# Output gates loaded with values and keys, POOL as a second DMA queue, and gate arithmetic in chunks of two

## The chip, the cores and the metric

The kernel runs on one core of a Trainium2 chip. Its time is the device time of one execution in microseconds (us). The engines of the core are named as the profile names them: PE is TensorE (PEld its weight loads), DVE is VectorE, ACT is ScalarE, POOL is GpSimd, SP is SyncE, which only issues DMAs here. Each engine works through its own instructions in the program's order and waits on semaphores for the others.

## The reference

An mLSTM-like attention over 4 batches, 8 heads and 768 steps with head size 40 is followed by a mixture of 8 experts, of which each of the 3,072 tokens takes two.

```python
for t in range(S):                                   # S = 768
    m_new = np.maximum(f_gate[:, :, t] + m, i_gate[:, :, t])
    f_stab = np.exp(f_gate[:, :, t] + m - m_new)
    i_stab = np.exp(i_gate[:, :, t] - m_new)
    C = f_stab * C + i_stab * outer(v_t, k_t)        # per batch and head, 40 x 40
    n = f_stab * n + i_stab * k_t
    denom = np.maximum(np.abs(n . q_t), 1.0)
    y[:, :, t] = sigmoid(o_gate[:, :, t]) * (C q_t) / denom
x = y as (3072, 320)
noisy = x @ w_gate + log1p(exp(x @ w_noise)) * noise
top2 of the 8 experts, weights softmax over the two
out[token] += weight * (relu(x @ w1[e]) @ w2[e])     # w1: 320 x 1024, w2: 1024 x 320
```

## The kernel before

The attention is done in chunks of 64 steps. A *unit* is one chunk of one pair of batches, so there are 2 x 12 = 24 units, and unit u gives 128 rows of x. The main loop runs over i = 0 to 23; iteration i finishes unit i and prepares units i+1 and i+2. The program's order is written out by hand, and a tile framework adds the semaphores.

In iteration i TensorE computes the state update (`c_part`, line 344), the output (`o_part`, line 353), the logits of the gates for unit i+2 (`e_part`, line 290, which reads the tiles LE and RE), the router's logits (line 398), the transpose of x of unit i-1 (`t_part`, line 378) and the scores of unit i+2 (`s_part`, lines 311 and 315, which read QK). ACT takes exponentials (line 293), the sigmoid of the output gate in place (`sig_part`, lines 298 to 300) and copies. DVE scales the keys (`k_part`, line 323, output kd), forms the weighted scores (`p_part`, lines 330 to 334) and divides by the denominator (`f_part`, lines 358 to 366, output tm). The product of tm with the sigmoid gives x (xr, line 367), on POOL up to unit 12 and on DVE after that.

Loads. `load_unit(u)` brings unit u into one of four buffers: queries and keys transposed (QK, line 141, two DMAs of 160 KB), values and keys in rows (VK, lines 143 and 144, two of 162 KB) and output gates (SG, line 146, one of 160 KB into one of five buffers). It is called for unit i+3 at the start of iteration i. `keep_rows(i-1)` then stores x of the unit before to a table in DRAM (line 370). All of these stand in SP's queue. So do the gates' rows: the recurrence of the forget and input gates is computed by DVE with scans along time (`gate_math`, lines 181 to 200) into the tile HL, first 128 steps, then 128, then 256 and 256 (the last 256 in portions of three instructions in iterations 1 to 3), and `gate_move` (lines 208 and 210, three DMAs for two units) brings HL's rows into LE and RE, every other iteration. From iteration 4 to 9 a piece of the first expert's w1 is loaded (lines 114 and 117) and from 6 to 11 split into a high and a low part by ACT and DVE (lines 133 and 134); pieces of w2 follow in iterations 13 to 16.

Before the loop TensorE runs 20 matmuls on zeros (`warm`, line 608), the scores of unit 0, four more on zeros, and the gates' logits of units 0 and 1. POOL blanks the rows of the four buffers that no load fills (`blank`, lines 160 to 163). ACT and DVE put columns of the identity into the buffers of units 0 to 3 (`keys`, lines 249 and 250). DVE makes a table of token numbers from constants (line 256).

From iteration 9 on groups of units are routed: DVE runs small steps between the others, and POOL scatters each token's number and weight into its expert's slots with indirect DMAs (line 562, two per unit). When 32 of them are issued (units 0 to 15), SP loads the first expert's slots (line 649), POOL gathers its tokens (line 663), TensorE transposes them (line 690), and the expert phase begins.

## Time and profile before

| | us |
|---|---|
| median of 3 runs | 587.41 |
| lowest, highest | 583.69, 587.6 |
| the profiled execution | 586.21 |
| its span, first to last instruction | 584.4 |

Busy time of the engines in the span: PE 547.4 (94%), PEld 497.5 (85%), DVE 341.3 (58%), ACT 252.0 (43%), POOL 226.5 (39%). TensorE's mean granted clock is 0.953 of the full speed. A matmul's end is modelled in the profile, so PE's share is not a measure of how much room is left; the stretches in which it waits are. Times of rows are counted from the span's start. The attention phase takes about the first quarter of the span, the eight experts the rest.

### The profile page before, as it was taken

To read this page: it belongs to the slowest core of one execution; us is meant where nothing else is said; L and a number is where in the kernel's file an instruction comes from. 1 tells how busy PE (TensorE), PEld (TensorE's weight loads), DVE (VectorE), ACT (ScalarE), POOL (GpSimd) and SP (SyncE) were. 2 spreads that over 40 slices of the span, in tenths; PEclk is the share of its full clock that TensorE was granted. 3 is DMA by queue.
4 is the path that set the end of the run, shared out by engine and by line. 5 is a ranking of instruction groups with operands and counts; after the bars stand their busy time and mean duration, and the time that the engine had idled before them with its cause. 6 is when DMAs were issued, how large, how long until landed. Compare 5 with 4: busy or idle time off the path is not lost. (4 is left out here: it accounts for less than half of the span.)

```text
span 584.4 us, 13268 instructions
## 1 busy us (share of the span) xinstructions
PE 547.4 (94%) x5098; PEld 497.5 (85%) x5099; DVE 341.3 (58%) x947; ACT 252.0 (43%) x612; POOL 226.5 (39%) x256
## 2 busy tenths in 40 slices
PE   8789888999799899999999999999999999999992
PEld 3678777888679798999899899989989988998992
DVE  8885648999774266663564465366356536635410
ACT  4667765877332154531551353254145225414300
POOL 7012111676545572434514424352442435241052
PEclk9789977999679799999999999999999999999997
DMA  6668887886273855544336345432634634241033
GB/s 163 154 167 229 220 223 203 239 208 165 84 252 112 268 73 138 153 109 67 76 102 148 50 139 135 48 91 82 148 61 125 144 42 128 48 45 14 1 41 37
DMA packets 47429, 72.07 MB, mean 123 GB/s; under 512 B 10290, under 2 KB 37115, under 8 KB 47344
## 3 DMA queue, kind: packets, MB, share of 16 engines
q1 hardware_dynamic: 35680, 54.36, 32.1%
q0 software_dynamic: 11680, 16.80, 18.2%
q8 instruction: 42, 0.69, 0.5%
q14 instruction: 27, 0.22, 0.1%
HBM read 53.47 MB, written 18.38 MB: 123 GB/s over the span
## 5 line engine op out<-in xcount | busy, mean ns | idle before, releaser
L858 POOL DMA_INDIRECT y_out<-y,mm x56 | 87.0, 1554 | 186.1 <-DVE y L848 185.4
L663 POOL DMA_INDIRECT xg<-rows,mm x56 | 58.5, 1044 | 61.0 <-DMA mm<-slots 30.2
L692 ACT ACTIVATE xh<-s 128x384 fp32r<-128x384 f32 (+1 forms) x56 | 25.9, 469 | 122.3 <-PE s L690 122.0
L817 PE MATMUL s<-xh,w1h 128*128 128x512 f32 (+1 forms) x255 | 77.8, 361 | 0.4 <-ACT xh L692 0.4
L823 DVE SCALAR_TENSOR_TENSOR hlo<-s,hh 128x512 fp32r<-128x512 f32 (+1 forms) x85 | 47.5, 559 | 43.6 <-ACT hh L822 43.2
L817 PE MATMUL s<-xh,w1l 128*128 128x512 f32 (+1 forms) x255 | 63.3, 357 | 0.0
L822 ACT ACTIVATE hh<-s 128x512 fp32r<-128x512 f32 (+1 forms) x85 | 41.8, 491 | 48.0 <-PE s L817 46.8
L562 POOL DMA_INDIRECT slots<-meta,ix x48 | 49.9, 1040 | 30.4 <-DVE ovm L557 16.6
L835 PE MATMUL o<-w2h,hh 128*128 128x320 f32 x176 | 55.7, 317 | 0.0
L835 PE MATMUL st<-w2h,hh 128*128 128x320 f32 x176 | 55.6, 316 | 0.0
L837 PE MATMUL st<-w2h,hlo 128*128 128x320 f32 x176 | 54.4, 309 | 0.0
L837 PE MATMUL o<-w2h,hlo 128*128 128x320 f32 x176 | 54.4, 309 | 0.0
L836 PE MATMUL st<-w2l,hh 128*128 128x320 f32 x176 | 54.4, 309 | 0.0
L836 PE MATMUL o<-w2l,hh 128*128 128x320 f32 x176 | 54.4, 309 | 0.0
L817 PEld LDWEIGHTS s<-xh,w1h 128*128 128x128 f32 x255 | 46.7, 192 | 6.7 <-ACT xh L692 0.6
L817 PEld LDWEIGHTS s<-xh,w1l 128*128 128x128 f32 x255 | 45.2, 191 | 5.8
L817 PE MATMUL s<-xl,w1h 128*128 128x512 f32 (+1 forms) x170 | 46.9, 357 | 0.0
L134 DVE TENSOR_TENSOR w1l<-raw,w1h 128x512 fp32r<-128x512 f32 (+1 forms) x48 | 33.3, 694 | 15.2 <-ACT w1h L133 14.5
L817 PE MATMUL e<-xh,w1h 128*128 128x320 f32 (+1 forms) x129 | 39.6, 361 | 0.0
L367 POOL TENSOR_TENSOR xr<-tm,sg 128x320 f32<-128x320 f32 x13 | 11.7, 904 | 68.6 <-DVE tm L366 20.1
L315 PE MATMUL s<-qk 64*64 64x64 f32 x768 | 36.6, 237 | 1.4 <-DMA qk<-qk_in 1.4
L353 PE MATMUL o<-vk,p 128*64 128x41 f32 (+2 forms) x768 | 32.3, 241 | 5.6 <-DVE p L334 3.6
(190 smaller groups left out, 1290.6 us busy)
## 6 DMA issues: line engine op xcount, KB each, us to landing
raw<-w_in SPq DMA_DIRECT2D x7, 1280.0 KB
vk<-vk_in SPq DMA_DIRECT2D x48, 162.0 KB
qk<-qk_in SPq DMA_DIRECT2D x48, 160.0 KB
raw<-w_in SPq DMA_DIRECT2D x7, 1024.0 KB
y_out<-zrow SPq DMA_DIRECT2D x15, 320.0 KB
raw<-w_in SPq DMA_DIRECT2D x18, 256.0 KB
sg<-og_in SPq DMA_DIRECT2D x24, 160.0 KB
rows<-xr SPq DMA_DIRECT2D x24, 160.0 KB
```

The source lines that it names most:

```text
L134: lo.tensor_sub(W1L[n, k, s], RAW1[n, k, s], W1H[n, k, s].bitcast(F32))
L315: T.matmul(SQ[u][p][half[p], h, :], q[r, 1, h, :], q[r, 0, h, :], start=True, stop=True)
L353: T.matmul(OQ[u][half[p], h, :], PP[u][p][n, h, :], VK[u % 4][p][n, h * 41:h * 41 + 41], start=True, stop=True)
L562: st = P.indirect_dma_start(out=MT, out_offset=bass.IndirectOffsetOnAxis(ap=ix[:, 2 * u + k:2 * u + k + 1], axis=0), in_=meta[:, u, k], in ...
L663: P.indirect_dma_start(out=XG[0:rows_of(t), t], out_offset=None, in_=XD[0:n], in_offset=bass.IndirectOffsetOnAxis(ap=token(e, t), axis=0), ...
L817: T.matmul(ps[:, 0:n], l, r, start=i == 0, stop=i == len(ops) - 1)
L822: A.activation(HH[:, f, c], ps[:, 0:m], AF.Relu)
L823: V.scalar_tensor_tensor(HLO[:, f, c], ps[:, 0:m], 0.0, HH[:, f, c].bitcast(F32), op0=OP.max, op1=OP.subtract)
L835: T.matmul(ps, HH[:, j, c], W2H[:, j], start=j == 0, stop=False)
L836: T.matmul(ps, HH[:, j, c], W2L[:, j], start=False, stop=False)
L837: T.matmul(ps, HLO[:, j, c], W2H[:, j], start=False, stop=j == 7)
L858: st = P.indirect_dma_start(out=out, out_offset=bass.IndirectOffsetOnAxis(ap=token(e, t), axis=0), in_=y[0:n], in_offset=None, compute_op= ...
```

## The change

Output gates no longer have a load of their own. A row of values and keys grows from 648 to 968 numbers and carries the gates of its half; the buffer of unit u is [128, 2, 968], and the gates are its columns 648 to 967 of the first part. So the gates have four buffers and not five, and the load of values and keys of unit i+3 overwrites the gates of unit i-1.

POOL's queue issues the moves of gates from the second on, up to iteration 12, and the stores of x of units 0 to 11; later ones stay on SP. Queries and keys of unit 0 are issued by ACT. The arithmetic of the gates is done by 128 steps throughout: 256 to 383 in iteration 0, 384 to 511 in iteration 1 and 512 to 767 in portions of four instructions in iterations 2 to 5. The identity columns of units 1 to 3 are put by POOL, those of unit 1 earlier than before, and POOL blanks the fourth buffer after the second move of gates. The four matmuls on zeros between the first scores and the first logits go. The pieces of w1 are loaded from iteration 6 and split from iteration 8, the pieces of w2 loaded from 14, and the zeros for the gathered rows written in iterations 6 to 12 (before: 4 to 10).

```diff
-W1LD, W1AT, W2AT = 4, 6, 13
+W1LD, W1AT, W2AT = 6, 8, 14
...
-    VKS = [att.tile([128, 2, 648], F32, name=f"vk{i}") for i in range(4)]
-    VK = [[t[:, p] for p in range(2)] for t in VKS]
-    SG = [att.tile([128, DM], F32, name=f"sg{i}") for i in range(5)]
+    VKS = [att.tile([128, 2, VW], F32, name=f"vk{i}") for i in range(4)]
+    VK = [[t[:, p, 0:648] for p in range(2)] for t in VKS]
+    SG = [t[:, 0, 648:VW] for t in VKS]
...
         if "v" in what:
-            SP.dma_start(VK[u % 4][0][0:64], vk[pr, c, 0])
-            SP.dma_start(VK[u % 4][1][64:128], vk[pr, c, 1])
-        if "o" in what:
-            SP.dma_start(SG[u % 5], og[:, u])
+            flat = VKS[u % 4].rearrange("p x c -> p (x c)")
+            SP.dma_start(flat[0:64, 0:VW], vk[pr, c, 0])
+            SP.dma_start(flat[64:128, 648:648 + VW], vk[pr, c, 1])
...
     blank(0, V)
+    load_unit(0, "k", A)
     blank(1, P)
...
     gate_move(0, (SP, P))
     blank(2, P)
-    blank(3, P)
...
     run(gate_math(GC * L, 256))
+    gate_move(1, (P, P))
+    blank(3, P)
     SP.dma_start(fit[:, :, 256:], fi[:, :, 256:])
     load_unit(1, "v")
-    load_unit(0, "o")
-    gate_move(1)
...
     keys(0, V, V)
+    keys(1, P, P)
...
     def keep_rows(u):
-        SP.dma_start(XD[128 * u:128 * u + 128], XR[u])
+        (P if u < XV - 1 else SP).dma_start(XD[128 * u:128 * u + 128], XR[u])
...
     s_part(0)
-    warm(WARM2)
     e_part(0, first=True)
     s_part(1)
     e_part(1, first=True)
-    keys(1, A, V)
     k_part(0)
     p_part(0)
-    keys(2, A, V)
-    keys(3, A, V)
+    keys(2, P, P)
+    keys(3, P, P)
...
         if i % 2 == 0 and i and i // 2 + 2 < 2 * GB:
-            gate_move(i // 2 + 2)
+            gate_move(i // 2 + 2, (P, P) if i < XV else (SP, SP))
...
         if i == 0:
-            run(gate_math(256, 512))
-            gate_move(2)
-            gates2 = gate_math(512, 768)
-        elif i < 4:
-            for _ in range(3):
+            run(gate_math(256, 384))
+            gate_move(2, (P, P))
+            gates2 = (s for t0 in (384, 512, 640) for s in gate_math(t0, t0 + 128))
+        elif i < 6:
+            for _ in range((8, 4, 4, 4, 4)[i - 1]):
                 next(gates2, None)
```

SP's queue in iteration 8 (the loads of unit 11) up to the first loads of iteration 9, before. The numbers behind the names are the buffers' own; qk_96 and vk_100 are the fourth buffers, raw holds the raw weights.

```order
L141 DMA qk_96<-qk_in 40x1024 x2
L143 DMA vk_100<-vk_in 64x648
L144 DMA vk_100<-vk_in 64x648
L146 DMA sg_102<-og_in 128x320
L370 DMA rows<-xr 128x320
L208 DMA le_87<-hl 32x2x64
L210 DMA re_85<-hl 1x16x128 x2
L114 DMA raw_113<-w_in 128x512
L141 DMA qk_93<-qk_in 40x1024 x2
```

And after, the same stretch:

```order
L143 DMA qk_96<-qk_in 40x1024 x2
L146 DMA vk_100<-vk_in 64x968
L147 DMA vk_100<-vk_in 64x968
L119 DMA raw_108<-w_in 64x512 x2
L143 DMA qk_93<-qk_in 40x1024 x2
```

The load of gates, the store of x and the three moves have left the queue, and the next unit's queries and keys follow the loads of this one and a piece of w1.

POOL's queue from the product of unit 7 to that of unit 9, before:

```order
L367 TENSOR_TENSOR xr<-tm,sg_103 128x320
L764 MEMSET xg 128x320
L367 TENSOR_TENSOR xr<-tm,sg_104 128x320
L764 MEMSET xg 128x320
L367 TENSOR_TENSOR xr<-tm,sg_105 128x320
```

And after:

```order
L370 TENSOR_TENSOR xr<-tm,vk_100 128x320
L766 MEMSET xg 128x320
L373 DMA rows<-xr 128x320
L212 DMA le_87<-hl 32x2x64
L214 DMA re_85<-hl 1x16x128 x2
L370 TENSOR_TENSOR xr<-tm,vk_97 128x320
L766 MEMSET xg 128x320
L373 DMA rows<-xr 128x320
L370 TENSOR_TENSOR xr<-tm,vk_98 128x320
```

The store of each unit and, in every other unit, three moves now stand between one product and the next.

POOL's queue at the start, after the blanking of the third buffer (vk_99), up to the first product, before:

```order
L160 MEMSET vk_100 32x328
L161 MEMSET vk_100 32x320
L162 MEMSET qk_96 32x1024
L163 MEMSET qk_96 32x1024
L255 MEMSET w1l 64x1024
L367 ISA
L367 TENSOR_TENSOR xr<-tm,sg_101 128x320
```

And after:

```order
L212 DMA le_88<-hl 32x2x64
L214 DMA re_86<-hl 1x16x128 x2
L162 MEMSET qk_96 32x1024
L163 MEMSET qk_96 32x1024
L164 MEMSET vk_100 32x328
L165 MEMSET vk_100 32x320
L251 COPY vk_98<-cs 40x320
L252 COPY vk_98<-cs 64x320
L251 COPY vk_99<-cs 40x320
L252 COPY vk_99<-cs 64x320
L251 COPY vk_100<-cs 40x320
L252 COPY vk_100<-cs 64x320
```

The second move of gates stands ahead of the fourth buffer's blanking, and the copies of identity columns (vk_98 is the buffer of unit 1, vk_100 that of unit 3) behind it; the memset of w1l and the first product follow.

## Rows read from the trace of the kernel before

**Rows 1.** Windows: us; busy PE, PEld, DVE, ACT, POOL; clock; DMA share; GB/s.
```profile
36.50:43.90 7.40, 6.01 (x121) 5.33 (x117) 5.70 (x13) 3.85 (x10) 0.87 (x1) 0.79 0.74 186
54.35:59.57 5.22, 4.73 (x121) 4.17 (x117) 2.22 (x6) 4.11 (x10) 1.18 (x2) 1.00 0.91 260
70.76:79.30 8.54, 6.20 (x121) 5.50 (x117) 4.40 (x11) 4.34 (x10) 1.17 (x2) 0.75 0.78 215
90.23:98.30 8.07, 7.69 (x111) 6.69 (x113) 7.91 (x43) 3.46 (x9) 1.24 (x2) 0.61 0.85 219
...
162.80:584.40 421.60, 407.15 (x2464) 379.40 (x2464) 213.35 (x514) 147.34 (x363) 160.88 (x178) 0.98 0.43 100
...
36.50:79.30 42.80, 35.92 (x787) 31.85 (x783) 26.09 (x62) 28.89 (x68) 7.93 (x13) 0.91 0.81 217
```

**Rows 2.** Waits of PE from 36.5 to 79.3: total us, times, longest.
```profile
PE s L311 <- DMA qk<-qk_in: 6.8, 6, 2.3
```

**Rows 3.** Timeline, units 8 and 9: start, us, engine; SP's issues, waiting scores.
```profile
68.78 0.79 SPq L141 DMA_DIRECT2D qk<-qk_in  x2
...
70.91 0.55 SPq L146 DMA_DIRECT2D sg<-og_in  x1
...
73.78 1.46 SPq L210 DMA_DIRECT2D re<-hl  x2
...
75.80 1.12 PE L311 MATMUL s<-qk,cs 64*64 64x512 f32 x2 [2.32 <-DMA qk<-qk_in]
...
76.22 0.98 SPq L141 DMA_DIRECT2D qk<-qk_in  x2
```

**Rows 4.** Timeline of PE at the start: first scores, first gate logits.
```profile
9.77 1.24 PE L315 MATMUL s<-qk 64*64 64x64 f32 x32 [1.36 <-DMA qk<-qk_in]
...
12.09 0.47 PE L290 MATMUL e<-re,le 98*128 98x512 f32 x1
```

**Rows 5.** Timeline of DVE at the start: gate arithmetic, constants, kd.
```profile
3.66 0.48 DVE L181 TENSOR_TENSOR_SCAN xg<-raw,xg 64x128 f32<-64x128 f32 x1
...
5.88 0.29 DVE L198 CAST hl<-xg 64x256 fp32r<-64x256 f32 x1
6.20 0.48 DVE L200 SCALAR_TENSOR_TENSOR hl<-hl,raw,xg 64x256 fp32r<-64x256 f32 x1
...
9.49 1.07 DVE L198 CAST hl<-xg 64x256 fp32r<-64x256 f32 x1
...
18.61 0.18 DVE L256 CAST toki<-cs 128x24 int32<-128x24 f32 x1 [2.16 <-DMA cs<-cst_in]
18.71 0.83 DVE L323 TENSOR_TENSOR kd<-vk,w 128x640 f32<-128x640 f32 x1
...
24.06 0.75 DVE L181 TENSOR_TENSOR_SCAN xg<-raw,xg 64x256 f32<-64x256 f32 x1
...
28.35 0.81 DVE L323 TENSOR_TENSOR kd<-vk,w 128x640 f32<-128x640 f32 x1
```

**Rows 6.** Timeline of POOL: a move of gates, memsets, a product, a long scatter.
```profile
7.00 0.73 POOL L210 DMA_DIRECT2D re<-hl  x1 [2.78 <-DVE hl L200]
...
9.47 0.94 POOL L163 MEMSET qk<- 32x1024 f32 x1
...
62.61 0.87 POOL L367 TENSOR_TENSOR xr<-tm,sg 128x320 f32<-128x320 f32 x1 [4.46 <-DVE tm L366]
63.41 0.38 POOL L764 MEMSET xg<- 128x320 f32 x1
...
108.37 1.61 POOL L562 DMA_INDIRECT slots<-meta,ix  x1 [0.31 <-issue]
```

**Rows 7.** Timeline of POOL at the end of the attention phase.
```profile
142.40 1.39 POOL L562 DMA_INDIRECT slots<-meta,ix  x1 [2.04 <-DVE ovm L557]
...
149.22 0.98 POOL L562 DMA_INDIRECT slots<-meta,ix  x1 [0.30 <-issue]
...
154.04 1.05 POOL L663 DMA_INDIRECT xg<-rows,mm  x1 [3.84 <-DMA mm<-slots]
```

More of the change, by code (lines that the diff above doesn't have):

```diff
@@ L46 @@
 GC = 2
+VW = 968
 KE = 98
-W1LD, W1AT, W2AT = 4, 6, 13
+W1LD, W1AT, W2AT = 6, 8, 14
 SC = ((20, 2), (NU, 3))
@@ L60, in build @@
 @with_exitstack
-def build(ctx, tc, qk, vk, og, fi, noise, wgn, w1, w2, cst, ce, rmask, vacant, out):
+def build(ctx, tc, qk, vk, fi, noise, wgn, w1, w2, cst, ce, rmask, vacant, out):
     nc = tc.nc
@@ L135, in split_w1, with load_unit @@
                 yield
-    def load_unit(u, what="kvo"):
+    def load_unit(u, what="kv", q=None):
         pr, c = divmod(u, NCH)
@@ L159, in blank @@
     def blank(i, q):
+        q.memset(QK[i][96:128], 0.0)
+        P.memset(QK[i][32:64], 0.0)
         P.memset(VK[i][1][32:64, 0:328], 0.0)
         P.memset(VK[i][0][96:128, 328:648], 0.0)
-        q.memset(QK[i][96:128], 0.0)
-        q.memset(QK[i][32:64], 0.0)
     blank(0, V)
+    load_unit(0, "k", A)
     blank(1, P)
@@ L169, in build @@
     SP.dma_start(cet, ce)
-    load_unit(0, "kv")
+    load_unit(0, "v")
     SP.dma_start(cs[:, C_CI:C_CI + 320], cst[:, C_CI:C_CI + 320])
@@ L182, in gate_math @@
         yield
-        gt = gts[t0 // 256 % 2][:, 0:n]
+        gt = gts[t0 // 128 % 2][:, 0:n]
         V.tensor_add(gt, f, mt[:, t0:t1])
@@ L189, in gate_math @@
         yield
-        ag = ags[t0 // 256 % 2][:, :, 0:n]
+        ag = ags[t0 // 128 % 2][:, :, 0:n]
         V.tensor_tensor_scan(ag[:, 1, :], rmt[:, 0:n], gt, 0.0, OP.mult, OP.add)
@@ L200, in gate_math @@
         V.scalar_tensor_tensor(HL[:, :, t0:t1], HL[:, :, t0:t1].bitcast(F32), rmt[:, 256:257], ag, op0=OP.mult, op1=OP.add)
+        yield
     GB = NCH // GC
@@ L295, in sig_part @@
     def sig_part(u):
-        g = SG[u % 5]
+        g = SG[u % 4]
         A.activation(g, g, AF.Exp, scale=-1.0)
@@ L366, in f_part @@
         V.tensor_mul(tm, ps[:, :, 0:D], dn[:, :, None].to_broadcast([128, H, D]))
-        (P if u < XV else V).tensor_mul(XR[u], tm.rearrange("p h d -> p (h d)"), SG[u % 5])
+        (P if u < XV else V).tensor_mul(XR[u], tm.rearrange("p h d -> p (h d)"), SG[u % 4])
     def keep_rows(u):
-        SP.dma_start(XD[128 * u:128 * u + 128], XR[u])
+        (P if u < XV - 1 else SP).dma_start(XD[128 * u:128 * u + 128], XR[u])
     XS = {}
@@ L762, in build @@
             next(pre1)
-        if 4 <= i < 11:
-            P.memset(XG[:, i - 4], 0.0)
+        if 6 <= i < 13:
+            P.memset(XG[:, i - 6], 0.0)
         for _ in range(at(SC, i)):
@@ L1050, in layout @@
         qk[:, :, 0, :, x] = a[:, :, 1]
-    vk = z(2, NCH, 2, L, 648)
+    vk = z(2, NCH, 2, L, VW)
     a = i["v"].reshape(2, 2, H, NCH, L, D).transpose(0, 3, 1, 4, 2, 5)
@@ L1054, in layout @@
     v[..., :D] = a
-    vk[..., :328] = v.reshape(2, NCH, 2, L, 328)
-    vk[..., 328:] = i["k"].reshape(2, 2, H, NCH, L, D).transpose(0, 3, 1, 4, 2, 5).reshape(2, NCH, 2, L, DM)
-    og = np.ascontiguousarray(i["o_gate"].reshape(2, 2, H, NCH, L, D).transpose(0, 1, 4, 3, 2, 5)).reshape(2, 128, NCH, DM)
-    og = np.ascontiguousarray(og.transpose(1, 0, 2, 3)).reshape(128, NU, DM)
+    k, og = [i[n].reshape(2, 2, H, NCH, L, D).transpose(0, 3, 1, 4, 2, 5).reshape(2, NCH, 2, L, DM) for n in ("k", "o_gate")]
+    for p in range(2):
+        vk[:, :, p, :, 320 * p:320 * p + 328] = v.reshape(2, NCH, 2, L, 328)[:, :, p]
+        vk[:, :, p, :, 320 * p + 328:320 * p + 648] = k[:, :, p]
+        vk[:, :, p, :, 648 * (1 - p):648 * (1 - p) + 320] = og[:, :, p]
     fi = np.stack([i["f_gate"].reshape(2, 1, 16, S), i["i_gate"].reshape(2, 1, 16, S)], 3)
```

5 lines of the change are left out of this document (2 added, 3 removed).

## The prediction

> **What bounds the kernel now.** I read the span by windows first, cut where a unit's output matmuls (line 353) begin, then the waits of TensorE, then the queue that the waits point to. From 162.8 us on, the expert phase runs 421.6 us with TensorE busy 407 and the clock at 0.98 [rows 1]. The change touches nothing there, so it can only move the point where that phase begins. Before it stand 24 attention units. A unit in which TensorE hardly waits costs 4.73 us of its work at the full clock (the window from 54.35: busy 4.73 of 5.22). But the seven units from 36.50 to 79.30 took 42.80, which is 6.11 each. In them TensorE waited six times, 6.8 us together, and each time for queries and keys still in flight [rows 2]. The two worst (windows from 36.50 and 70.76, 7.40 and 8.54 us) also ran at a mean granted clock of 0.79 and 0.75, so matmuls cost more as well. Seven units at 4.73 would be 33.1: 9.7 us lie here, 6.8 in waits and 2.9 in clock and small waits.
>
> Why are the loads late? The SP queue issues everything, in order. One turn begins with the two qk loads of unit 11 at 68.78, and those of unit 12 begin at 76.22: 7.44 us a turn, against 4.73 that TensorE needs [rows 3]. The first four issues took 2.13 us (68.78 to 70.91). The sg load, the x store, the three moves of gates and a piece of w1 fill the other 5.3, waits among them. In such a turn SP falls behind TensorE, and at 75.80 TensorE has stood 2.32 us for the qk issued at 68.78.
>
> **The change part by part.**
>
> *SP's queue, units 3 to 9.* The sg load goes into the vk rows, and the store of x and three moves of gates every other unit go to POOL. Per unit SP keeps four issues (2.13 us) and in six units a piece of w1 (two issues at most, as long as two qk: 0.79), 2.9 us against 4.73. It then waits for buffers to come free. The new wait is that vk of unit i+3 overwrites the gates of unit i-1, so it needs POOL's product xr of unit i-1; the next unit's qk is queued behind it. That product began at 62.61 and took 0.87 [rows 6] in unit 7, so vk of unit 11 could be issued at 63.5 and qk of unit 12 about 1.2 us later, where they went out after 69.57 and at 76.22 [rows 3]. The wait added thus ends 6 us before the issue of that vk and 11 before that of the qk in the old order, and the user of that qk comes two units later. I therefore let all six waits go: up to -9.7. What is next late? DVE has 26.1 us of work in these 42.8 [rows 1]; the gates' steps of units 3 to 5 (four steps each, about 1.5 us) bring a DVE turn near 4.85, 0.1 a unit over TensorE. The transfers: a unit moves 320 + 484 + 160 KB, 0.99 MB, and 1.25 with a piece of w1, which at the 260 GB/s of the best window [rows 1] is 4.80 us. Both take back 0.7 together. Term: **-9.0**, between -3.0 (transfers stay slow, below) and -9.7.
>
> The Trainium skill's "Perfetto Trace Analysis", section "What 'DMA-bound' means", lists the DMA engines and the issuing sequencer as two different bounds. SP's 7.44 us a turn speak for the sequencer, and the DMA share of 0.81 in the same stretch says that the engines are not far from it [rows 1, 3]; by the first the term is -9.0, by the second its small end.
>
> *Start, units 0 to 2.* Queries and keys of unit 0 leave on ACT's queue, the four extra warm matmuls go, the identity columns of units 1 to 3 and the second move of gates go to POOL. TensorE's first scores started at 9.77 after 1.36 of waiting for qk, and the first e matmul at 12.09 [rows 4]. Without the wait and the 1.04 us of warm matmuls both come about 2 us earlier. That is not yet the end's gain, because DVE is next. It waited 2.16 us for constants that stood behind the gates and sg on SP (line 256, 18.61), then did kd of unit 1 at 18.71 [rows 5]. Those stood behind an sg load (0.55) and three moves (1.46 for two) [rows 3] that now leave SP, so they come 2 to 2.5 us earlier. But kd of unit 1 waits for POOL: three moves of gates from about 11, at 0.73 (the one that POOL issues already) to 0.98, with 0.30 of issue [rows 6, 7], so 3.1 to 3.8; the blanking of the fourth buffer, two memsets of 0.94 and two near 0.38 [rows 6], 2.6; two copies of 320 columns, which no row of POOL shows, between the 0.38 of a memset as wide and the 0.87 of a product with two inputs [rows 6], so 0.8 to 1.8. End: 17.5 to 19.2; I take 18.0, as a copy reads one input only: 0.7 earlier. Then the gates' arithmetic: a chunk of 256 held DVE from 24.06 to 28.35, 4.29 us; one of 128 went from 3.66 to 6.68, 3.0 [rows 5]. So kd of unit 2 gains another 1.3. A whole chunk of 128 after unit 1 takes 3.0 where three of the eight steps of 256 took 1.6 in proportion, which gives 1.4 back, hidden in part by TensorE. Over all 24 units DVE does four chunks of 3.0 where there were two of about 4.2, 3.6 us more, spread over six units; of it I count only what the unit times above hold. Term by the start of unit 3: **-1.2**, range 0 to -2.5.
>
> *POOL.* It takes over 12 stores and 8 moves of three: 36 DMAs. Nothing in the trace shows such a store on POOL. The nearest rows are its scatter of 128 rows, 0.98 with 0.30 idle before it, 1.61 at worst, and its direct move, 0.73 [rows 6, 7]. At 1.28 a pair of units costs POOL two products of 0.87, two memsets of 0.38 in units 6 to 12 and five DMAs: 8.9 us of the 9.46 that TensorE takes for two. So they fit, with little room, and xr of the even units comes about 1.4 us later than its inputs. TensorE reads that xr a unit later, after some 3 us more. Price: 0; it becomes a rival if a DMA costs more. The scatters themselves begin later, at unit 13, and the stores are back on SP then.
>
> The Trainium skill's "SBUF — State Buffer", section "Who interferes with whom", says that a DVE copy or cast in its fast mode and a GpSimd operation shut each other out for the whole instruction, descriptor writing included, which speaks against moving work to POOL. The trace agrees that they collide: the cast of one chunk took 0.29 alone and 1.07 when it started with POOL's memset of 0.94 [rows 5, 6]. By that rule each of the 36 DMAs could wait for a cast of at most 0.3 to 0.4 us, in the few units that have one; the sum stays, since POOL's 0.5 us of room per pair covers it.
>
> *Pieces of w1 two units later.* Their splitting on DVE (0.7 each for 512 columns, in proportion to kd's 0.83 for 640 [rows 5]) now falls on units 12 and 13, in the stretch from 90.23 where DVE was busy 7.91 of 8.07 us [rows 1]. One piece lands in a unit with idle DVE, one not: **+0.5**, between 0 and +1.4. The half-speed clock there (0.61) stays.
>
> *The end of the attention phase.* The experts' first gather began at 154.04. It waits for the last of six scatters, issued at 149.22; the first of these, at 142.40, had POOL idle for 2.04 us until DVE's routing of units 13 to 15 was done [rows 7]. So the gather follows the units, with 2.04 us to spare over POOL's earlier scatters, and moves with them.
>
> **Sum:** -9.0 - 1.2 + 0.5 = -9.7. The profiled execution took 586.2 us, its span 584.4; 586.2 - 9.7 = 576.5. The runs shown have a median of 587.4 (583.7 to 587.6), and the profiled one stands 1.2 below it; I split the difference: **577 us**. About 1%, 5.9 us, is what a measurement of this kernel can tell from no change.
>
> **The rivals.**
>
> 1. *The transfers are the bound, not SP's issue.* The same bytes must pass, and the stretch moved them at 217 GB/s with the engines 0.81 busy [rows 1]. If units 6 to 11 with w1 stay at that rate, a unit takes 1.25 MB / 217 = 5.75 us, 6 x 1.0 more than forecast: 583. For it: the qk issued at 68.78 had not landed 6 us later, with other loads beside it [rows 3]. Against it: 260 GB/s in one window, and larger rows in place of the sg rows of 1,280 bytes.
>
> 2. *POOL becomes the bound, and the time ends above the old one.* If a DMA on POOL costs d, a pair costs 2.5 + 5d; it exceeds 9.46 from d = 1.39, and eats the whole 9.7 us over five and a half pairs from d = 1.74. With d = 2.0, the worst scatter and its issue (1.61 + 0.30 [rows 6, 7]) rounded up, it is 12.5 a pair, +3.0 x 5.5 = +16.7: 593. xr then holds up vk, and qk behind it. For it: nine tenths of POOL are filled by the plan already, and a move that waits for TensorE to be done with the gates' buffer keeps the next xr behind it. Against it: 0.73 for the one direct move in the trace.
>
> 3. *The waits only move, to DVE.* The chunk after unit 1 and the four steps after each of units 2 to 5, stretched by POOL as the cast of 1.07 was [rows 5], hold five units at 5.4 in place of 4.85: 2.8 less gained, and the start gives nothing, another 1.2: 581. For it: DVE works 26.1 of 42.8 us already [rows 1]; against it, that leaves 2.4 us a unit.
>
> **How the numbers follow.** Forecast 0.58 (its own range is 572 to 580.5; the low end is 577 with the start at -2.5, nothing given back by w1, and the unit from 90.23 at the full clock, some 3 us), rival 1 0.20, rival 3 0.09, rival 2 0.12, and 0.01 for anything else. The range of 571 to 587 takes in rivals 1 and 3 and leaves out rival 2 and the edges. Faster by over 1% means below 581.5: the forecast and most of rival 3, 0.65. Within 1%: rival 1, the rest of rival 3 and what is left over, 0.23. Slower: rival 2, 0.12.
>
> **What would show it.** Right: the windows of units 4 to 10 near 4.8 us at clock 1.00, no wait of the scores' first matmuls (line 311) for qk above 0.3 us, SP waiting for POOL's xr; kd of unit 1 near 18, of unit 2 near 26; POOL's store near 1 us; the gather at about 144.5. Wrong: POOL stores of 1.5 us or more, with t of a unit waiting for xr; qk waits that persist with the DMA share above 0.9; or kd of unit 1 held by POOL's copies beyond 19.

## The result, and the profile after

The changed kernel takes 579.94 us (median of 6 runs, 577.32 to 583.08), the kernel before, in as many runs beside it, 586.69 (583.69 to 590.77). The ratio is 0.9883 with a 95% interval of 0.9835 to 0.9932: 6.8 us faster, where 577 had been forecast. The profiled execution took 578.57 us with a span of 576.7, against 586.21 and 584.4. Lines of the changed kernel stand one to three higher than before: output 356 (353), scores 314 and 318 (311 and 315), logits 293 (290), kd 326 (323), xr 370 (367), store 373 (370).

Where the 7.7 us of the two spans come from, read at the starts of the output matmuls of units 3, 10, 14 and 23 and of the experts' first matmul:

| stretch | before | after | difference | forecast |
|---|---|---|---|---|
| start to unit 3 | 36.50 | 40.28 | +3.8 | -1.2 |
| units 3 to 9 | 42.81 | 33.97 | -8.8 | -9.0 |
| units 10 to 13 | 24.00 | 22.36 | -1.6 | } +0.5 |
| units 14 to 22 | 46.28 | 47.74 | +1.5 | } |
| unit 23 to the experts | 13.22 | 12.87 | -0.4 | 0 |
| experts | 421.6 | 419.5 | -2.1 | 0 |

The windows of the changed kernel, cut as in [rows 1], with two more: 12 to 26, and the first 4.2 us of the experts (columns: us; busy PE, PEld, DVE, ACT, POOL; clock; DMA share; GB/s).

```profile
0.00:40.28 40.28, 30.95 (x438) 22.22 (x440) 29.15 (x80) 20.30 (x40) 23.41 (x42) 0.79 0.78 176
12.00:26.00 14.00, 10.89 (x167) 8.69 (x168) 8.08 (x23) 7.42 (x15) 8.99 (x15) 0.55 0.94 194
40.28:74.24 33.96, 33.41 (x784) 29.59 (x781) 25.13 (x64) 27.00 (x64) 16.06 (x28) 1.00 0.88 247
85.12:91.85 6.73, 6.35 (x111) 5.60 (x113) 6.67 (x39) 3.65 (x10) 3.84 (x8) 0.75 0.64 180
157.20:161.40 4.20, 4.20 (x19) 3.41 (x19) 3.59 (x13) 1.53 (x5) 3.29 (x4) 1.00 0.51 178
157.20:576.70 419.50, 404.81 (x2464) 377.67 (x2463) 213.53 (x514) 146.88 (x363) 160.98 (x178) 0.98 0.43 100
```

The kernel before, in three stretches that were not shown:

```profile
0.00:36.50 36.50, 28.82 (x441) 20.04 (x444) 31.00 (x75) 21.58 (x43) 13.80 (x23) 0.91 0.64 157
12.00:26.00 14.00, 10.12 (x194) 8.36 (x194) 11.01 (x29) 8.89 (x19) 3.69 (x4) 0.80 0.80 184
162.80:167.00 4.20, 4.20 (x11) 3.33 (x12) 1.89 (x9) 0.98 (x4) 3.08 (x4) 0.50 0.61 206
```

In units 3 to 9 TensorE is now busy 33.41 of 33.96 us at the full clock, and the waits for queries and keys [rows 2] are gone. This is the whole list of PE's waits there that count:

```profile
PE st L347 <- issue: 0.5, 1, 0.5
```

SP's timeline of the changed kernel, where [rows 3] showed a turn of 7.44 us, has turns of 4.39 and 5.72, each with a stop of 1.7 to 3.0 us ahead of a load of values:

```profile
65.07 0.89 SPq L143 DMA_DIRECT2D qk<-qk_in  x2
67.61 0.47 SPq L146 DMA_DIRECT2D vk<-vk_in  x1
...
69.46 0.80 SPq L143 DMA_DIRECT2D qk<-qk_in  x2
73.25 0.47 SPq L146 DMA_DIRECT2D vk<-vk_in  x1
...
75.18 0.75 SPq L143 DMA_DIRECT2D qk<-qk_in  x2
```

What it stops for stands in SP's waits from 40 to 74 us (us in total, times, longest): the buffer whose gates POOL still reads in xr, or the memset just behind xr. SP, the engine that was always late, now waits 13.7 us in seven units and TensorE does not notice.

```profile
SPq L146 <- POOL xg L766: 9.0, 4, 2.8
SPq L146 <- POOL xr L370: 4.7, 3, 1.9
```

The start went the other way. The outputs of units 0 to 3 begin at 18.13, 26.12, 31.89 and 40.28, before at 15.18, 24.80, 31.06 and 36.50. So of the 3.8 us only 0.8 are there at unit 2, and 3.0 come in the one unit behind it. PE at the start, as in [rows 4]: the first scores come at 8.20 (before 9.77), but the first logits only at 11.39, and two more waits of about 2 us follow, for queries and keys of unit 1 and for the gates of unit 4. The granted clock is at half, the lower of its two levels (1.2 and 2.4 GHz), from 13.3 to 26.9 us and from 37.2 to 40.6, each time behind such waits; before, up to unit 3, only from 20.4 to 27.2.

```profile
8.20 1.15 PE L318 MATMUL s<-qk 64*64 64x64 f32 x32
11.39 0.47 PE L293 MATMUL e<-re,le 98*128 98x512 f32 x1 [2.04 <-ACT le L224]
...
14.14 2.06 PE L318 MATMUL s<-qk 64*64 64x64 f32 x32 [2.05 <-DMA qk<-qk_in]
...
35.36 0.47 PE L293 MATMUL e<-re,le 98*128 98x512 f32 x1 [1.83 <-DMA re<-hl]
```

The constants of the logits, ce, that ACT needs first, land 2.5 us later than before, although SP issued them at 2.13 in both kernels; what is new beside them is 320 KB of queries and keys that ACT issued from 1.73 on. The first line is the kernel before, the second the changed one.

```profile
5.49 0.52 ACT L220 ACTIVATE le<-raw 98x384 fp32r<-98x384 f32 x1 [3.45 <-DMA raw<-ce_in]
7.98 0.52 ACT L224 ACTIVATE le<-raw 98x384 fp32r<-98x384 f32 x1 [5.94 <-DMA raw<-ce_in]
```

DVE there, as in [rows 5]: 1.17 us for rmask, which SP had issued just ahead of ce, then 4.75 for constants (before 2.16), so kd of unit 1 comes at 20.81 (18.71) and of unit 2 at 29.16 (28.35).

```profile
6.25 0.42 DVE L194 TENSOR_TENSOR_SCAN xg<-raw,xg 64x128 f32<-64x128 f32 x1 [1.17 <-DMA raw<-rmask_in]
...
20.63 0.18 DVE L259 CAST toki<-cs 128x24 int32<-128x24 f32 x1 [4.75 <-DMA cs<-cst_in]
20.81 0.82 DVE L326 TENSOR_TENSOR kd<-vk,w 128x640 f32<-128x640 f32 x1
...
29.16 0.82 DVE L326 TENSOR_TENSOR kd<-vk,w 128x640 f32<-128x640 f32 x1
```

POOL, as in [rows 6] and [rows 7]: the move of gates for units 4 and 5 at 29.67, a pair of turns in the middle, and the end of the attention phase, where POOL still waits for DVE's routing (3.35) and the gather that began at 154.04 begins at 148.59.

```profile
29.67 0.60 POOL L212 DMA_DIRECT2D le<-hl  x1 [5.41 <-PE e L293]
...
52.44 0.87 POOL L370 TENSOR_TENSOR xr<-tm,vk 128x320 f32<-128x320 f32 x1 [2.89 <-DVE tm L369]
53.60 0.57 POOL L373 DMA_DIRECT2D rows<-xr  x1 [0.30 <-DVE p L337]
55.49 0.57 POOL L212 DMA_DIRECT2D le<-hl  x1 [1.32 <-PE st L347]
56.05 0.98 POOL L214 DMA_DIRECT2D re<-hl  x2
...
136.86 1.39 POOL L565 DMA_INDIRECT slots<-meta,ix  x1 [3.35 <-DVE ovm L560]
...
148.59 1.08 POOL L664 DMA_INDIRECT xg<-rows,mm  x1 [3.92 <-issue]
```

### The profile page after: what moved, and what is told of

Same layout as the page of the kernel before. It is cut to its first block, busy times and chain, and to the rows that moved or that the text cites. A ratio compares the mean times of both kernels' runs of the same rounds, so it can differ in the third digit from the quotient of the medians.

```text
span 576.7 us, 13267 instructions
## 1 busy us (share of the span) xinstructions
PE 542.3 (94%) x5095; PEld 493.6 (86%) x5095; DVE 340.4 (59%) x959; ACT 250.0 (43%) x609; POOL 248.1 (43%) x299
## 5 line engine op out<-in xcount | busy, mean ns | idle before, releaser
L356 PEld LDWEIGHTS o<-vk,p 128*64 128x64 f32 (+2 forms) x768 | 28.6, 147 | 9.8 <-DVE p L337 2.9
```

The lines of the kernel that those rows point to most:

```text
L356: T.matmul(OQ[u][half[p], h, :], PP[u][p][n, h, :], VK[u % 4][p][n, h * 41:h * 41 + 41], start=True, stop=True)
```

## Experiments

Two theories were to be told apart for units 3 to 9: A, that SP's turn of issues was the bound, and rival 1 of the prediction, that the transfers were. For POOL it was the price of a DMA (rival 2), and for the start, which of its edits costs 3.8 us.

The experiments ran in three groups, each on another chip, and on each of the three the kernels took 6 to 7% longer than in the first measurement, the kernel before too (medians 624.32, 626.2 and 625.85). So a ratio is taken only to the kernel before of the same group, and of the profiles only the first 95 us are compared (what happens behind that is told at the end). For scale, the changed kernel, run again in the second group, had 0.9922 [0.9889, 0.9954].

Each measurement of a kernel has one profile, and profiles of one kernel differ. The two of the changed kernel have the output of unit 3 at 40.28 and 39.09 and units 3 to 9 at 33.97 and 34.89. Five kernels of the table whose program is the same up to the output of unit 0 have that output at 17.91 to 19.95. So at unit 3 a difference of less than 2 us between two profiles shows nothing.

| kernel | group | ratio [95%] | output of unit 3 at | units 3 to 9 | output of unit 10 at |
|---|---|---|---|---|---|
| before (first measurement) | | 1 | 36.50 | 42.81 | 79.31 |
| changed (first measurement) | | 0.9883 [0.9835, 0.9932] | 40.28 | 33.97 | 74.25 |
| gates in the rows only | 1 | 0.9973 [0.9935, 1.0011] | 37.15 | 40.05 | 77.20 |
| POOL's issues only | 1 | 0.9930 [0.9901, 0.9959] | 38.59 | 33.82 | 72.41 |
| both of these | 1 | 0.9966 [0.9930, 1.0001] | 36.28 | 37.66 | 73.94 |
| changed, matmuls on zeros back | 1 | 0.9918 [0.9885, 0.9950] | 41.03 | 34.33 | 75.36 |
| changed, first qk on SP | 2 | 0.9932 [0.9902, 0.9963] | 41.69 | 32.88 | 74.57 |
| changed, third move on SP | 2 | 0.9965 [0.9931, 0.9998] | 39.26 | 36.79 | 76.05 |
| changed, old start | 2 | 0.9950 [0.9917, 0.9982] | 36.23 | 37.10 | 73.33 |
| changed, again | 2 | 0.9922 [0.9889, 0.9954] | 39.09 | 34.89 | 73.98 |
| changed, token table later | 3 | 0.9873 [0.9823, 0.9922] | 38.66 | 32.60 | 71.26 |
| the same, gate arithmetic early | 3 | 0.9870 [0.9834, 0.9906] | 40.80 | 32.62 | 73.42 |
| the same, qk of unit 1 early | 3 | 0.9895 [0.9852, 0.9939] | 40.14 | 33.81 | 73.95 |
| changed, more work on POOL | 3 | 0.9951 [0.9922, 0.9980] | 40.69 | 36.12 | 76.81 |

**Gates in the rows of values and keys, nothing else changed.**

```diff
-    SG = [att.tile([128, DM], F32, name=f"sg{i}") for i in range(5)]
+    SG = [t[:, 0, 648:VW] for t in VKS]
...
-        if "o" in what:
-            SP.dma_start(SG[u % 5], og[:, u])
```

> The kernel before with one part of the change: the output gates ride in the rows of values and keys; stores of x, moves of gates, the start and the gates' arithmetic stay as they were, SP issues everything. Theory A (SP's issue and its order were what made queries and keys late): one of seven and a half issues per unit goes, so half or less of the waits in units 3 to 9 goes, 6.8 us to 3 to 5, and the time falls by 2 to 4 us. Theory B (the transfers were the bound and the longer rows cure them): nearly all of the waits go, as in the changed kernel, -6 to -9 us. Theory C (neither): no change.

The time is that of before within its interval. Units 3 to 9 take 40.05, and PE waited three times for queries and keys, 4.4 us together, the longest at 73.83 for those of unit 11. SP's timeline shows why: it issued them at 66.78, 3.4 us after the output of unit 8 had begun (63.38), and a turn still lasts 7.02 us.

```profile
66.78 0.83 SPq L142 DMA_DIRECT2D qk<-qk_in  x2
...
73.80 0.69 SPq L142 DMA_DIRECT2D qk<-qk_in  x2
```

Before, the same issue came 3.8 us after the output of unit 8 (68.78 [rows 3] against 65.00). Of the 6.8 us of waits 4.4 are left, as theory A had it, and theory B falls; the 2 to 4 us of time that A expected are not shown.

**POOL issues the stores and the moves of gates from unit 6 on, nothing else changed.**

```diff
-        SP.dma_start(XD[128 * u:128 * u + 128], XR[u])
+        (P if u < XV - 1 else SP).dma_start(XD[128 * u:128 * u + 128], XR[u])
...
-            gate_move(i // 2 + 2)
+            gate_move(i // 2 + 2, (P, P) if i < XV else (SP, SP))
```

> The kernel before with the other part: POOL issues the stores of x of units 0 to 11 and the moves of gates from the fourth on up to iteration 12; output gates keep their own load and five buffers, the start is the old one. Theory A: two and a half of seven and a half issues per unit leave SP, the waits for queries and keys in units 3 to 9 go to under 1 us and the time falls by 6 to 9 us. Theory B (transfers and row length): the same bytes in the same rows, so the waits stay at 5 us or more and the time falls by under 2 us. If POOL were near its limit, the product of x would come late and TensorE would wait at the transpose of x.

This alone is faster, by 0.7%, and units 3 to 9 take 33.82, as in the changed kernel, with a wait of 0.4 us left of the six. The program's transfers are those of before, byte for byte and row for row: the sg loads of 1,280 bytes a partition are still there. Window, then PE's wait for queries and keys in it (one more of 0.7 is put down to nothing):

```profile
38.59:72.40 33.81, 32.68 (x787) 29.03 (x783) 23.71 (x56) 28.26 (x67) 16.30 (x29) 1.00 0.91 251
```

```profile
PE s L311 <- DMA qk<-qk_in: 0.4, 1, 0.4
```

Queries and keys of unit 11 are now issued at 62.02, 0.6 us ahead of the output of unit 8 (62.63).

```profile
62.02 0.73 SPq L141 DMA_DIRECT2D qk<-qk_in  x2
...
70.41 0.65 PE L311 MATMUL s<-qk,cs 64*64 64x512 f32 x2 [0.38 <-DMA qk<-qk_in]
```

They took 8.4 us to land, where those of before took 7.0 (68.78 to 75.80 [rows 3]). So the transfer of a load became no shorter; it was issued earlier against its use. In this stretch theory A holds, and rival 1, that the transfers stay at 217 GB/s, falls: they went at 251 once SP was relieved. With a DMA share of 0.91 the engines are not far off as the next bound.

The output of unit 3 begins 2.1 us later than before, though the start is nearly the old one. From the output of unit 2 on it took 8.19 us, with no wait above 1.0 but at half clock from 31.3 to 38.1.

**Both of these, with the start, the chunks and the pieces of w1 of before** (the two diffs together).

> The kernel before with both parts on the steady units and the old start (unit 0's queries and keys on SP, the four warm matmuls, identity columns by ACT and DVE, second and third move of gates on SP, chunks of 256, w1 from iteration 4). Theory A: units 3 to 9 take 33 to 34.5 us instead of 42.8, and the start costs what it did before, so the time is below the changed kernel's: 574 to 578 (-9 to -12 against before). Theory D (the changed start helps after all, and its loss in the profile is compensated later): this is slower than the changed kernel, 581 to 585.

Units 3 to 9 take 37.66, with one wait of 1.25 for queries and keys and one gap of 1.76 that is put down to nothing. The time (0.9966) isn't distinguishable from either part's. Fusing adds nothing to POOL's issues that these runs can show. SP's wait for POOL, 13.7 us in the changed kernel, is 1.5 us, once, in this one.

**The changed kernel with the four matmuls on zeros put back.**

```diff
     s_part(0)
+    warm(WARM2)
     e_part(0, first=True)
```

> The changed kernel with the four matmuls on zeros between the first scores and the first gate logits put back. In the changed kernel's profile the clock was at its lower level from 13.3 to 26.9 us, for 13.7 us where it had been 6.8. Theory E (the missing matmuls let the clock fall): the low stretch shrinks to 7 us or less and the time falls by 1.5 to 3 us. Theory F (it is the waits for the constants ce at 11.39 and for the keys of unit 1 at 14.14, 2.0 us each, that let it fall): no change within 1 us, since the second wait stays.

They don't save the clock: it is low from 13.5 to 27.2 us, as in the changed kernel (13.3 to 26.9), and the waits stay, for the first logits and for unit 1's queries and keys. The ratio, 0.9918, is the changed kernel's: theory F.

```profile
12.57 0.47 PE L293 MATMUL e<-re,le 98*128 98x512 f32 x1 [1.77 <-DMA re<-hl]
...
15.39 1.42 PE L318 MATMUL s<-qk 64*64 64x64 f32 x21 [2.11 <-DMA qk<-qk_in]
```

**The changed kernel with queries and keys of unit 0 back on SP.**

```diff
-    load_unit(0, "k", A)
     blank(1, P)
...
-    load_unit(0, "v")
+    load_unit(0, "kv")
```

> The changed kernel with queries and keys of unit 0 back on SP's queue, behind rmask and ce. Theory: the changed start is late because the early 320 KB held up rmask and ce; then line 194 no longer waits for rmask (1.17 us in the changed kernel), hl is ready about 1.2 us earlier, the output of unit 3 begins near 39 (40.28 in the changed kernel, 36.50 before), and the time is about 1 us lower than the changed kernel's. Rival: the constants behind the larger rows of values, and POOL's late moves, set the start; then kd of unit 1 stays near 20.8, the output of unit 3 stays near 40.3 and the time is the changed kernel's within 0.5 us.

The wait for rmask is gone, and ce lands early again:

```profile
5.91 0.52 ACT L223 ACTIVATE le<-raw 98x384 fp32r<-98x384 f32 x1 [3.87 <-DMA raw<-ce_in]
```

So the first move of gates, which overwrites rows of le, leaves SP at 6.71 (changed kernel 8.53, again 9.48, before 6.75), queries and keys of unit 1 leave at 8.17 (10.00, 10.95, before 8.22), and TensorE waits 0.41 us for them instead of 2.05. That much of the start the early 320 KB do cost. But the first logits still wait, now 2.75 us for the move of gates (12.31), kd of unit 1 comes at 20.14, and the output of unit 3 begins at 41.69 and not near 39: units 2 and 3 ran at half clock (21.8 to 42.3). The theory is right about the waits and its gain is not there at unit 3; there the rival had it right, and the ratio (0.9932) is the changed kernel's (0.9922) within its interval.

**The changed kernel with the move for units 4 and 5 back on SP.**

```diff
-            gate_move(2, (P, P))
+            gate_move(2)
```

> The changed kernel with the move of gates for units 4 and 5 (issued in iteration 0) back on SP. Theory: POOL reaches that move only after the product of unit 0 and its copies, its transfer then lands late among SP's loads, and the logits of unit 4 wait 1.83 us for it and leave the clock low after; then that wait is gone, units 2 to 3 take about 6 us and not 8.4, the output of unit 3 begins near 38, and the time is about 2 us lower. Rival: DVE's arithmetic and the previous readers of the buffer set that move, whichever queue issues it; on SP it then stands ahead of queries and keys of the next units, the output of unit 3 begins at 40 or later, and the time is the same or up to 1 us higher.

Units 2 to 3 take 5.85 us instead of 7.13 in the changed kernel of the same group, and the wait for that move is gone. The output of unit 3 begins at 39.26, no earlier than the 39.09 there, but this profile was 1.45 us later at unit 2 (33.41 against 31.96), 0.87 of that at the output of unit 0, which the edit does not reach. So a gain of up to 1.3 us at unit 3 is neither shown nor excluded. And SP pays. After the loads at 23.78 its queue stands until 30.62, because the move needs DVE's arithmetic, and then three units' loads leave within 7 us; their queries and keys come 1.23 us late at 43.73, and units 3 to 9 take 36.79. The theory was right about the wait; the 2 us of time that it expected are not there, and the ratio (0.9965 against 0.9922, overlapping) is if anything worse.

```profile
23.78 0.47 SPq L147 DMA_DIRECT2D vk<-vk_in  x1
30.62 0.68 SPq L212 DMA_DIRECT2D le<-hl  x1
...
32.62 0.88 SPq L143 DMA_DIRECT2D qk<-qk_in  x2
```

**The changed kernel with the start of before** (the two edits above, the matmuls on zeros, identity columns by ACT and DVE, the fourth buffer blanked early, the second move on SP).

```diff
-    gate_move(1, (P, P))
-    blank(3, P)
...
-    keys(1, P, P)
...
+    keys(1, A, V)
...
-    keys(2, P, P)
-    keys(3, P, P)
+    keys(2, A, V)
+    keys(3, A, V)
```

> The changed kernel with the start of the kernel before: queries and keys of unit 0 on SP, the four matmuls on zeros, identity columns by ACT and DVE, the fourth buffer blanked early, moves of units 2 to 5 on SP; later moves and the stores stay on POOL, gates stay in the rows of values, arithmetic stays by 128 steps. Theory: the loss of 3.8 us up to unit 3 comes from these edits and is independent of the gain after; then the output of unit 3 begins at 36.5 to 37.5, units 3 to 9 still take 34 to 35, and the time is about 3 us below the changed kernel's, ratio to before near 0.983. Rival: what is won early is lost to the later units, because the transfers must be worked off either way; then units 3 to 9 take 37 or more and the ratio is 0.987 to 0.99, as the changed kernel's.

The output of unit 3 is back at 36.23, so these edits together do cost the start 2.9 us (39.09 in the same group). Yet units 3 to 9 take 37.10, unit 10 begins only 0.65 earlier, and the time is no better (0.9950, overlapping the changed kernel's 0.9922). That is the rival: most of what is won is given back at once, here.

```profile
32.00 0.88 SPq L143 DMA_DIRECT2D qk<-qk_in  x2
...
41.37 0.65 PE L312 MATMUL s<-qk,cs 64*64 64x512 f32 x2 [1.88 <-DMA qk<-qk_in]
```

Those queries and keys, of unit 5, are the second of three pairs that left SP within 4.5 us (29.79, 32.00, 34.20), and they took 9.4 us to land.

**The changed kernel again** (no edit).

> The changed kernel itself, beside the others. If nothing depends on the chip: 0.988 of the kernel before, between 0.983 and 0.993.

0.9922, within the range expected, and 0.4% nearer to 1 than in the first measurement; the intervals overlap.

**The table of token numbers later.**

```diff
-        V.tensor_copy(toki, cs[:, C_TOK:C_TOK + NU])
...
         if i == 6:
+            V.tensor_copy(toki, cs[:, C_TOK:C_TOK + NU])
```

> The changed kernel with the table of token numbers (line 259) made in iteration 6 instead of ahead of kd of unit 1. Theory: the 4.75 us for which DVE waits there for constants hold kd of unit 1; without them kd of unit 1 begins near 18 (20.81 in the changed kernel), when POOL's copies are done, the output of unit 1 near 24 (26.1), that of unit 3 at 38 to 39 (40.28), and the time is 1 to 2 us lower. Rival: kd is held by something that comes at the same time (values of unit 1, POOL's copies), or the late move of gates for units 4 and 5 takes the gain back; then the output of unit 3 stays at 40 and the time does not change.

DVE's wait for constants is gone and kd of unit 1 begins at 19.36, behind POOL's copies. But the output of unit 1 begins at 28.26, later than the 26.12 of the changed kernel: the logits of unit 2 now wait 2.72 us for the move of gates that POOL issued from 14.06 on.

```profile
22.57 0.76 PE L292 MATMUL e<-re,le 98*128 98x512 f32 x1 [2.72 <-DMA re<-hl]
```

The third move of gates, issued at 28.21, holds nobody here, and the output of unit 3 begins at 38.66, which is not to be told from the 39.09 of the changed kernel again. From unit 3 on each unit takes 4.65, and unit 10 begins at 71.26, the earliest of all. Its ratio, 0.9873, is below the 0.9922 of the second group, but the intervals overlap.

**The same, with the arithmetic of steps 256 to 383 and its move ahead of the loop.**

```diff
     keys(3, P, P)
+    run(gate_math(256, 384))
+    gate_move(2, (P, P))
     constants()
...
         if i == 0:
-            run(gate_math(256, 384))
-            gate_move(2, (P, P))
```

> The same, and the arithmetic of steps 256 to 383 with its move of gates comes ahead of the loop, into the time in which DVE waited for constants. Theory: this takes 3.0 us of DVE out of iteration 0 and brings the move of units 4 and 5 forward from 29.7 to about 20; kd of unit 1 begins at 19 to 20, the output of unit 3 near 35 (40.28 in the changed kernel), no logits wait for that move, units 3 to 9 take 34 as in the changed kernel, and the time is 4 to 5 us below the changed kernel's, ratio to before 0.981 to 0.985. Rival: what the start gains is given back by unit 10 as in the kernel with the old start, because queries and keys come too late for units 3 to 5; then the output of unit 10 begins at 73.5 or later (74.25 in the changed kernel) and the time is the changed kernel's within 1 us.

The arithmetic fills DVE's idle time as meant (17.09 to 20.61) and the third move goes at 22.19 and not at 29.67. The output of unit 3 still begins at 40.80, not near 35. The logits of unit 2 wait 2.33 us as in the kernel before this one, and the half clock now lasts without a break:

```profile
12.00:37.00 25.00, 19.85 (x304) 16.21 (x305) 19.55 (x51) 12.27 (x26) 14.12 (x24) 0.52 0.90 202
```

The expected 4 to 5 us were not there at unit 3; the theory that DVE alone sets the start falls. The ratio, 0.9870, overlaps the changed kernel's.

**The same, with queries and keys of unit 1 ahead of the first move of gates.**

```diff
+    load_unit(1, "k")
     V.memset(mt[:, 0:1], -1e30)
...
     gate_move(0, (SP, P))
     blank(2, P)
-    load_unit(1, "k")
```

> The same as the one before, and queries and keys of unit 1 are issued ahead of the first move of gates, not behind it. Theory: the first scores of unit 1 no longer wait for them (2.05 us in the changed kernel), the output of unit 0 begins near 16 (18.13), that of unit 3 near 33, and the time is 1 to 2 us below the kernel without this edit. Rival: the earlier 320 KB delay the first move of gates and the constants, the logits of unit 0 wait longer, and the output of unit 0 begins at 17.5 or later.

The scores of unit 1 no longer wait; the first logits do, 5.58 us, with the move of gates now behind 320 KB. The output of unit 0 begins at 19.13: the rival. The ratio, 0.9895, is no better than the 0.9870 without this edit.

```profile
14.11 0.77 PE L292 MATMUL e<-re,le 98*128 98x512 f32 x1 [5.58 <-DMA re<-hl]
```

**The changed kernel with 1.9 us more work on POOL per unit** (two memsets on a tile that nobody reads, behind each store of units 0 to 11).

```diff
+        if u < XV - 1:
+            P.memset(idle, 0.0)
+            P.memset(idle, 0.0)
```

> The changed kernel with two more memsets of 32x1024 on POOL behind each of the stores of units 0 to 11, about 1.9 us more work a unit and no transfer. Theory: a DMA costs POOL 0.6 to 0.9 us, so that it waits 2.9 us for tm before a product and has room for them; the time stays within 1 us of the changed kernel's. Rival, the price of the prediction (1.28 a DMA, 8.9 of 9.46 us in a pair of units, 0.5 to spare): 3.8 more a pair then makes POOL the bound, 3.2 us a pair, over five and a half pairs 17 us slower, ratio to before near 1.02.

POOL's product waits 0.36 to 1.85 us for its inputs instead of 2.9, and the stretch takes 36.12 against 34.89 and 33.97, some 1.2 to 2.1 us more; the ratio is 0.9951. So POOL had room for nearly all of this load, and the 17 us that the price of 1.28 a DMA implied do not come. Whether the theory's "within 1 us" holds is open: 0.9951 and the changed kernel's 0.9922 are some 1.8 us apart, with overlapping intervals.

```profile
53.99 0.57 POOL L374 DMA_DIRECT2D rows<-xr  x1 [0.30 <-POOL xr L371]
54.55 1.03 POOL L376 MEMSET idle<- 32x1024 f32 x1
55.64 0.94 POOL L377 MEMSET idle<- 32x1024 f32 x1
...
58.43 0.88 POOL L371 TENSOR_TENSOR xr<-tm,vk 128x320 f32<-128x320 f32 x1 [0.36 <-ACT w L297]
```

None of these kernels is shown to beat the changed one; the two lowest ratios are those with the token table later. Nor is the changed kernel (0.9922 again, 0.9883 first) shown to beat the one with POOL's issues only (0.9930), whose edit is two lines. The rest of the change, the rows, the start, the chunks and w1, has no gain in time that these runs show.

## Why the prediction was right, and where it was not

*SP's queue, units 3 to 9: the mechanism was right, the size in part luck.* Forecast -9.0, measured -8.8. The waits for qk are gone, the new wait of SP for xr is there and costs nothing, and DVE does not become late (no wait of PE for it in the stretch). That it was SP's issue and not the transfers is shown by POOL's issues alone: the same transfers, issued earlier, and the same -9. The gates in the rows, which the prediction counted with the rest, do not by themselves show a gain. The Trainium skill's "Perfetto Trace Analysis", section "What 'DMA-bound' means", names the DMA engines and the issuing sequencer as separate bounds. In units 3 to 9 the runs show the second; at the start, below, the DMA share speaks for the first.

But the prediction added this term to that of the start as if they did not touch. The two kernels with POOL's issues that reached unit 3 as early as before (36.28 and 36.23) took 37.66 and 37.10 for units 3 to 9, so that the term was -5.1 and -5.7 there; in these profiles about -9 came only where unit 3 began some 2 us later or more. The number to trust is the place of unit 10: forecast 10.2 us earlier, measured 5.1 (79.31 to 74.25).

*Start: the term that failed.* Forecast -1.2, range 0 to -2.5; measured +3.8. Three steps of it failed, each by taking a transfer that is issued earlier, or by another engine, for one that lands in time.

First, queries and keys of unit 0 on ACT's queue: first scores and first logits were to come "about 2 us earlier". The scores came 1.6 earlier, but ce landed 2.5 later, the logits gained 0.7, and with SP held at the first move of gates the queries and keys of unit 1 were issued 1.8 later and waited for. With that edit taken back (first qk on SP) the delay of ce and that of unit 1's queries and keys are gone.

Second, the constants, which "stood behind an sg load" and three moves "that now leave SP, so they come 2 to 2.5 us earlier". They were indeed issued earlier, the three from 12.81 on and not from 14.28, but they landed 2 us later (20.63, before 18.61). POOL's copies, which were to hold kd of unit 1 until 18.0, were done with its buffer at 17.6; that estimate was right. By the output of unit 2 all that is lost is 0.8 us.

Third, the move of gates for units 4 and 5, which the change also gives to POOL and which the term does not price. POOL issued it at 29.67, the logits waited for it until 35.36, and the clock fell behind that: unit 2 to unit 3 took 8.39 us where it had been 5.44, 3.0 of the 3.8. Where that move went from SP (third move on SP) or was issued earlier by POOL (the three kernels from the token table later on), no logits waited for it and this unit took 4.7 to 5.9. How much of the 3.0 is the wait and how much the clock is open: the kernel with POOL's issues only took 8.19 there with the move on SP.

Why the transfers landed late is argued, not shown. From 12 to 26 us the DMA share is 0.94, against 0.80 before, though the engines moved only 194 GB/s, less than the 247 at a share of 0.88 in units 3 to 9. The gates of units 0 and 1 ride in the rows of values there, and the loads of unit 2's values leave SP 2.3 us earlier (15.61, before 17.95). Over all kernels the order is the same: the five with the old start have shares of 0.78 to 0.87 in that window and the output of unit 3 at 36.2 to 38.6, the nine with the new one or most of it 0.90 to 0.94 and 38.7 to 41.7. No run took bytes out of the stretch. The experiments fit a stretch in which an earlier issue only moves who waits: with the constants out of the way the second move of gates is late; with qk of unit 1 early the first move is late; with the old order SP's loads pile up behind unit 3. The two costs of it are in the windows: to the output of unit 3 TensorE idles 9.3 us where it was 7.7, and is busy 30.95 where it was 28.82, at a mean clock of 0.79 instead of 0.91. The four matmuls on zeros that went are not shown to be a cause: with them back the start was no earlier (41.03). What a start without any of these waits would give was not reached by any kernel here.

How much of the 3.8 us a better start could bring in is open: the old start kept 0.65 of its 2.9 us at unit 10, and the token table later had 2.7 us there (73.98 to 71.26), with a ratio that its interval does not separate from the changed kernel's.

*POOL: the price of nothing was right, and the DMA cheaper than assumed.* 1.28 was taken for each; the store takes 0.57 to 0.60 and up to 0.30 before it, two small moves 0.98. The five DMAs of a pair of units are 2 x 0.58 + 0.57 + 0.98 = 2.7 and not 6.4, and with the 2.5 of products and memsets the pair is 5.2 of 9.3 us, under 7 with 0.30 of idle ahead of each DMA. The kernel with 3.8 more a pair fills POOL to 9.0, and even there the stretch grew by some 2 us at most. Rival 2 was further off than its 0.12 said.

*w1 two units later.* Forecast +0.5, measured -1.6 in units 10 to 13 and +1.5 in units 14 to 22, -0.2 together. The unit in which the routing and the splitting meet went from 8.07 us to 6.73, at a clock of 0.75 instead of 0.61, with DVE still busy 6.67 of it. Units 14 and 15 took 5.82 and 5.18 where it had been 5.15 and 4.66, and the output of unit 15 waits 0.85 us for DVE. No kernel here moved w1 alone, so which edit these belong to is not shown.

*End and experts.* The gather follows the units, as forecast: 5.5 us earlier, where 9.5 were forecast; the miss of the start is more than the difference. "The change touches nothing there" held for the work of the experts but not for their clock: in the kernel before the half clock lasted 4.2 us into that phase, in the changed one it was over when it began (0.50 and 1.00 in the windows of 4.2 us), which by this count of the clock is the 2.1 us. That it was over is a matter of where the phase falls, and no run shows that it would always be.

So -9.7 became -7.7: the start missed by 5.0, and w1, the end and the clock of the experts gave 3.1 that were not counted. That the time came out so near to 577 is luck to that extent: with the start and the queue as measured and the rest as forecast, the sum is -4.5 and the time near 582, outside the forecast's own range of 572 to 580.5 and next to rival 1's 583.

## What to carry to other kernels

Ask for each stretch whether the issuing queue or the transfers bound it before moving a DMA: with a DMA share of 0.81 and an issue turn longer than TensorE's unit, a second queue took up to 9 us out of a stretch, and with a share of 0.94 each earlier load went with another that was late. A transfer that is issued earlier does not land earlier by that alone: look at what it will share the engines with. When a queue is the bound, move the DMAs that nobody waits for (the stores) to an engine that idles, and check that engine's time before each wait rather than its busy share. A gain at the front is only a gain if the stretch behind it can take the work earlier; look for the place where it is given back.

## What the runs showed of the hardware that was not expected

- A direct store of 160 KB occupies POOL 0.57 to 0.63 us, less than an indirect one of 128 rows (0.98), and two small moves of gates 0.98.
- The cast of the token numbers is recorded with 0.18 us in the changed kernel and with 0.97 where POOL's memset of 0.95 ran beside it (kernel with the matmuls on zeros). The Trainium skill's "SBUF — State Buffer", section "Who interferes with whom", says that a DVE cast in a mode that uses two ports and a GpSimd instruction lock each other out for the whole of an instruction. The lengths agree; but kd, DVE's next instruction, began 0.18 us behind the cast in both kernels, so here that instruction lost nothing by it.
- Moves that POOL issued at 14.06 to 15.6 us held a matmul until 22.57, with SP's loads in flight beside them: the 96 packets of the queue that POOL issues to moved from 16.51 to 21.30. The first move, issued by SP at 8.67 and by POOL, held the logits until 11.45 (kernel with the token table later).
- The constants ce, which SP issues at 2.13 us, landed at 7.98 to 9.42 in the eight profiles in which ACT issued the 320 KB of unit 0's queries and keys (from 1.73 on in the changed kernel), and at 5.20 to 5.91 in the six in which SP issued the same bytes behind ce.
- In the three later groups, TensorE issued one or a few matmuls every 0.7 to 2.1 us at half clock, waiting for nothing that the profile shows, in stretches between 95 and 157 us, while the DMA share was 0.15 to 0.25 (windows from 106 to 122 of two kernels). All profiles of those groups have it, and neither profile of the first measurement. From the output of unit 14 to the experts the changed kernel took 97.7 us there and 60.6 in the first measurement, which is 37 of the 42 us by which its median is longer there; why it occurs is not known. PE of the kernel with POOL's issues only:

```profile
109.51 0.23 PE L353 MATMUL o<-vk,p 104*64 104x41 f32 x1 [1.18 <-issue]
111.62 0.43 PE L353 MATMUL o<-vk,p 128*64 128x41 f32 x3 [0.49 <-issue]
```
